# The second network's first layer as 2x2 block products by one level of Strassen's algorithm, with weights converted in pairs

## The chip, the core and the metric

One core of a Trainium2 chip runs the whole program. The metric is device microseconds of one execution, from launch to the end on the core; lower is better. Of the core's engines four compute: TensorE (PE: matmuls, results in PSUM; its weight loads are listed as PEld), VectorE (DVE), ScalarE (ACT) and GpSimd (POOL). SyncE's queue (SP) issues the transfers. Each engine works through its own queue in order, and an instruction whose semaphores have not been raised holds back everything behind it on that engine.

## What is computed

```python
def reference(q, k, v, w1, b1, w2, moe_..., moe2_...):
    x = _attn_ref(q, k, v, w1, b1, w2)      # B=2, H=8, S=576, D=64, bias by a small network
    x = x.transpose(0, 2, 1, 3).reshape(1152, 512)
    g = x @ w_gate; val = x @ w_val         # 512 -> 1536, the first network
    x = (silu(g) * val) @ w_out             # 1536 -> 512
    h = x @ w_in                            # 512 -> 2048, the second network's first layer
    return softplus(h) @ w_out2             # 2048 -> 512
```

The weights of both networks come as float64. Each product is made of three matmuls of a shorter kind (fp32r), which read operands that were rounded to it: for a = ah + al and b = bh + bl the kernel adds ah bh, ah bl and al bh.

## The kernel before

The core runs attention first, whose queues are written out by hand, then two networks on all 1152 tokens at once. X lies transposed, 512 features in four tiles of 128 partitions, tokens along the columns, as a high part `xh` and a low part `xl`.

**Weights.** `units` lists 68 blocks of 512 x 128 (or 128 x 512) float64 weights in the order of use: 24 for gate and value, 12 for the first network's output, and twice 8 for `w_in` with 8 for `w_out2`. `stages` (L511 to L531) turns one into float32 by bits and splits it: ScalarE scales the upper words by 2^-112 (L523), VectorE shifts left by 3 (L525), puts the sign bit back (L526) and adds three bits of the lower word (L528), ScalarE rounds to the high part `wh` (L530), GpSimd subtracts to get the low part `wl` (L531). `convert` and `weights` keep this some blocks ahead of their use; `ring` holds 9 blocks.

**Products.** `products` (L546) issues, for one block and one range of 384 tokens, 4 x 3 = 12 matmuls of 384 columns into one PSUM buffer (L552). The first network runs 12 feature blocks, each with gate and value on three token ranges; ScalarE's Silu, VectorE's product and `split` (high part L557 on ScalarE, low part L558 on VectorE) give `gh` and `gl`. Its output layer makes four rows of blocks, three weight blocks each, and `split` gives the next X, again as high and low part.

**Second network.** In two halves of 8 feature blocks: for each block and each token range 12 matmuls, Softplus (L609), `split` to `g2h` and `g2l`; then for each of nine blocks of 128 tokens 8 x 3 matmuls of 512 columns (L619), the result copied to or added to `acc` by VectorE (L623, L625), and in the second half sent out (L626). PSUM is 8 buffers of one bank (`psM`). Outside attention a scheduler orders each engine's queue ahead of the run, from the program's order and its own estimates; buffers are waited for tile by tile.

Of the kernel before, what the change touches and what calls it, by code (L numbers as in the profile page):

```python
# [19 lines left out]
P = 128  # L20
# [6 lines left out]
RING = 9  # L27
# [65 lines left out]
def tile_kernel(ctx: ExitStack, tc, qT, kT, vS, wb, wg, wv, wo, wi, wo2, table, out):  # L93
# [9 lines left out]
    def new_x():  # L103
        return [xp.tile([P, NK, NT], F32R, tag=t, name=t) for t in ("xh", "xl")]
# [8 lines left out]
    with ExitStack() as actx:  # L113
# [372 lines left out]
    units = []  # L486
    for f in range(FF1 // P):
        units += [col_block(wg, f), col_block(wv, f)]
    for m in range(NK):
        for fb in range(FF1 // P // NK):  # L490
            units.append(row_block(wo, fb, m))
    for hf in range(2):
        units += [col_block(wi, 8 * hf + f) for f in range(8)]
        units += [rows(wo2, 8 * hf + f) for f in range(8)]
    NU = len(units)

    mpool = opener(ctx)
    rawp = mpool("rawp", 3)
    cvp = mpool("cvp", 2)
    ring = mpool("ring", RING)  # L500
    wk = mpool("wk", 2)
    psM = mpool("psM", 8, space=PSUM)
    loaded, ready = [], []

    def load(n):
        while len(loaded) < min(n, NU):
            raw = rawp.tile([P, NK, P, 2], I32, tag="raw", name="raw")
# [156 lines left out]
```

## Time and profile before

| | |
|---|---|
| median of 3 runs | 620.9 us (620.18 to 623.96) |
| the profiled execution, its own time | 624.0 us |
| its span, first to last instruction | 622.2 us |
| TensorE busy | 606.4 us, 97% |
| VectorE / ScalarE / GpSimd busy | 391.5 / 312.3 / 195.9 us |
| first matmul of the first network | 195.58 us |
| first matmul of the second network | 420.60 us |
| last matmul starts | 618.24 us |

The profile is one execution on the chip. Busy time is the union of an engine's instructions; since matmuls overlap in the record (each lasts about twice its share), the pace of TensorE is read from the starts of successive matmuls, not from their durations. The same holds, less so, for VectorE and ScalarE, whose next instruction may start some 0.09 us before the last has ended.

### The profile page before, as it was taken

Reading aid. Unit: us, or ns where it says so; the run is one execution under the profiler, and the core shown is the slowest. Engines: PE = TensorE matmul, PEld = TensorE weight load, DVE = VectorE, ACT = ScalarE, POOL = GpSimd, SP = SyncE. Lnnn points to the kernel's source line nnn. Section 1 sums busy time; section 2 is a strip of 40 time slices with the busy share of each in tenths; the row PEclk is TensorE's granted clock in tenths of the full one; section 3 lists DMA queues with packets and bytes.
Section 4 is the critical chain, followed back from the end, with each engine's and each line's share of the span. In section 5 each row is a group of like instructions: output and inputs, shape, how many; then the busy total and the mean of one; then the engine's idle time right before and its main releaser. Section 6 shows DMA issues by size and latency. Waiting matters only on the chain.

```text
span 622.2 us, 10920 instructions
## 1 busy us (share of the span) xinstructions
PE 606.4 (97%) x4032; PEld 542.7 (87%) x4032; DVE 391.5 (63%) x849; ACT 312.3 (50%) x623; POOL 195.9 (31%) x231
## 2 busy tenths in 40 slices
PE   8899799999999999999999999999999999999997
PEld 5343588888888999999999999999998889999886
DVE  7999779999978996567566534325644017965111
ACT  5988767777776453434533332226662003675000
POOL 0301668888853441131121221212220004421000
PEclk9999889999999999999999999999999999999999
DMA  9879624444333553323323232323232003520111
GB/s 240 206 195 204 157 73 108 104 107 109 94 103 102 170 169 102 103 68 102 102 69 110 94 102 73 97 68 95 76 101 67 1 1 96 169 75 1 52 51 52
DMA packets 47413, 63.29 MB, mean 102 GB/s; under 512 B 4480, under 2 KB 35200, under 8 KB 47360
## 3 DMA queue, kind: packets, MB, share of 16 engines
q1 hardware_dynamic: 47360, 62.59, 35.6%
q8 instruction: 32, 0.52, 0.4%
q14 instruction: 21, 0.17, 0.1%
HBM read 49.60 MB, written 2.36 MB: 84 GB/s over the span
## 4 chain that ended last, share of the span: by engine, by line
PE 90%; DMA 3%; DVE 3%; ACT 2%; issue 1%; SPq 0%; POOL 0%; DVEq 0%; ACTq 0%; POOLq 0%
PE pm L552 52%; PE pm L619 16%; PE po L374 7%; PE ps L282 7%; PE pt L346 5%; PE pb L245 3%; DMA bias<-st 2%; DVE r L237 2%; ACT st L257 1%; PE warm L454 1%; DMA vt<-in_vS_dram 1%; ACT r L235 0%; PE ps L346 0%; SPq L142 0%; ACT at L354 0%
## 5 line engine op out<-in xcount | busy, mean ns | idle before, releaser
L531 POOL TENSOR_TENSOR wl<-x,wh 128x512 fp32r<-128x512 f32 x68 | 90.6, 1340 | 288.8 <-ACT wh L530 170.4
L552 PE MATMUL pm<-xh,wl 128*128 128x384 f32 x480 | 160.5, 334 | 0.0
L552 PE MATMUL pm<-xh,wh 128*128 128x384 f32 x480 | 160.4, 334 | 0.0
L552 PE MATMUL pm<-xl,wh 128*128 128x384 f32 x480 | 160.3, 334 | 0.0
L523 ACT ACTIVATE u<-raw 128x512 f32<-128x512 f32 x68 | 45.9, 675 | 107.1 <-DVE x L526 58.4
L552 PEld LDWEIGHTS pm<-xh,wh 128*128 128x128 f32 x480 | 90.1, 188 | 0.4 <-issue 0.4
L552 PEld LDWEIGHTS pm<-xh,wl 128*128 128x128 f32 x480 | 90.1, 188 | 0.3 <-POOL wl L531 0.3
L552 PEld LDWEIGHTS pm<-xl,wh 128*128 128x128 f32 x480 | 90.1, 188 | 0.0
L525 DVE TENSOR_SCALAR x<-u 128x512 int32<-128x512 int32 x68 | 41.5, 610 | 69.0 <-POOL wl L531 68.4
L530 ACT CAST wh<-x 128x512 fp32r<-128x512 f32 x68 | 42.1, 619 | 84.3 <-PE pm L619 40.2
L320 POOL TENSOR_SCALAR e<-e,sm 128x576 f32<-128x576 f32 x64 | 49.0, 766 | 41.0 <-DVE sm L319 28.9
L528 DVE SCALAR_TENSOR_TENSOR x<-raw,x 128x512 int32<-128x512 int32 x68 | 55.9, 822 | 1.5
L619 PE MATMUL pm<-wh,g2l 128*128 128x512 f32 x144 | 56.1, 389 | 0.0
L619 PE MATMUL pm<-wl,g2h 128*128 128x512 f32 x144 | 56.1, 389 | 0.0
L619 PE MATMUL pm<-wh,g2h 128*128 128x512 f32 x144 | 56.0, 389 | 0.0
L526 DVE SCALAR_TENSOR_TENSOR x<-u,x 128x512 int32<-128x512 int32 x68 | 54.0, 794 | 1.5
L245 PE MATMUL pb<-r,wb_sb 128*32 128x288 f32 x576 | 48.8, 412 | 6.1 <-ACT st L257 4.6
L317 ACT ACTIVATE e<-e,sm 128x576 f32<-128x576 f32 x64 | 49.9, 780 | 7.5 <-DVE sm L303 6.4
L282 PE MATMUL ps<-kst,ql 128*128 128x288 f32 x160 | 49.5, 338 | 4.2 <-DVE sm L318 2.3
L237 DVE TENSOR_SCALAR r<-G 128x576 f32<-128x576 f32 x108 | 51.4, 550 | 0.1
L303 DVE CUSTOM_DVE_ANT_0 e<-ps,bias 128x576 f32<-128x576 f32 x64 | 47.8, 747 | 2.1 <-ACT st L257 1.2
L245 PEld LDWEIGHTS pb<-r,wb_sb 128*32 128x32 f32 x576 | 20.2, 109 | 32.9 <-ACT st L257 13.6
(76 smaller groups left out, 1049.2 us busy)
## 6 DMA issues: line engine op xcount, KB each, us to landing
raw<-in_wo_dram SPq DMA_DIRECT2D x28, 512.0 KB, 3.5
bias<-st SPq DMA_DIRECT2D x32, 288.0 KB, 4.5
raw<-in_wi_dram SPq DMA_DIRECT2D x16, 512.0 KB, 3.7
raw<-in_wg_dram SPq DMA_DIRECT2D x12, 512.0 KB, 3.6
raw<-in_wv_dram SPq DMA_DIRECT2D x12, 512.0 KB, 3.6
kr<-in_kT_dram SPq DMA_DIRECT2D x16, 288.0 KB, 4.3
qr<-in_qT_dram SPq DMA_DIRECT2D x16, 288.0 KB, 4.3
v<-in_vS_dram SPq DMA_DIRECT2D x8, 384.0 KB, 4.9
```

The lines of the kernel that those rows point to most:

```text
L237: nc.vector.tensor_scalar(r, G[:, w0 : w0 + S], PB[:, n : n + 1], 0.0, op0=ALU.add, op1=ALU.max)
L245: nc.tensor.matmul(pb[32 * ct : 32 * ct + 32, hf, :HALF], W2, rs[ct][:, HALF * hf : HALF * (hf + 1)], start=True, stop=True,)
L282: nc.tensor.matmul(ps[:, hf, :HALF], u[t][:, o : o + P], kst[:, a, HALF * hf : HALF * (hf + 1)], start=i == 0, stop=i == len(parts) - 1,)
L303: nc.vector.tensor_tensor_reduce(out=e[:, :S].rearrange("p (a n) -> p a n", a=2), in0=ps[:, :, :HALF], in1=bt.rearrange("p (a n) -> p a n" ...
L317: nc.scalar.activation(e, e, AF.Exp, bias=sm[:, 0, n : n + 1], scale=-1.0, accum_out=sm[:, 1, n : n + 1])
L320: nc.gpsimd.tensor_scalar(e, e, sm[:, 3, n : n + 1], 1.0, op0=ALU.mult, op1=ALU.mult)
L523: nc.scalar.activation(u, hw.bitcast(F32), AF.Copy, scale=2.0**-112)
L526: nc.vector.scalar_tensor_tensor(x, ui, -(2**31), x, op0=ALU.bitwise_and, op1=ALU.bitwise_or)
L528: nc.vector.scalar_tensor_tensor(x, lw, 29, x, op0=ALU.logical_shift_right, op1=ALU.bitwise_or)
L531: nc.gpsimd.tensor_tensor(wl, x.bitcast(F32), wh.bitcast(F32), op=ALU.subtract)
L552: nc.tensor.matmul(ps[:, :n], w[:, k], x, start=first and k == 0 and i == 0, stop=last and k == NK - 1 and i == 2)
L619: nc.tensor.matmul(ps, g, w.rearrange("p k f -> p (k f)"), start=f == 0 and i == 0, stop=f == 7 and i == 2)
```

## The change

**Strassen.** The first layer of the second network, h = x @ w_in, is cut into 2 x 2 blocks: features in halves of 256, tokens in halves of 576, and output features in eight pairs of 128. For each pair (a *quad*) seven block products replace eight, in the form with shared sums (Winograd's): S1 to S4 are sums of weight blocks, T1 to T4 sums of X blocks. Each product is 2 x 3 x 2 = 12 matmuls of 288 columns (L702), the two halves of 576 columns in two banks of one buffer. Buffers of PSUM are now 4 of two banks (`wide`). The products x1 to x7 of a quad accumulate in three buffers a, b, c: x1 in a; c starts as a copy of a (L739, ScalarE); x5 and x3 in b; x6, x7 and x4 in c; results of b and c are kept (L728) and added (L722) where two outputs share them.

**Order.** TensorE's queue in the second network is written out by hand as words: x and y are the two quads of a round, z the next round's first, the digit the product, c a sum; t and u are the two halves of a block of tokens' output matmuls. There are four rounds of 2 quads and 4 x 128 features instead of two halves of 8 x 128. All other engines are still ordered by the scheduler.

**X.** The output layer of the first network writes X in full (`xf`, L654), and its blocks B and sums T, with high and low parts, are made as its rows finish (L619 to L628, L658 to L679).

**Weights.** They are converted two blocks at a time (`as_float`, 1024 columns; the first two pairs in halves). For the first network ScalarE's Prelu with slope -2^32 does the scaling and the sign in one instruction (L530), which takes out the sign instruction on VectorE; `w_in` and `w_out2` still have it (L535). The low parts are made by VectorE (`split`, L541); GpSimd has no instruction left behind attention. The ring holds 4 pairs, 6 in the second network. A quad also makes its four sums on VectorE (L558 to L561). The two explicit table loads are gone; ScalarE's queue has a load before the first Silu and before the first Softplus.

```diff
-        nc.scalar.activation(u, hw.bitcast(F32), AF.Copy, scale=2.0**-112)
-        nc.vector.tensor_scalar(x, ui, 3, None, op0=ALU.logical_shift_left)
-        nc.vector.scalar_tensor_tensor(x, ui, -(2**31), x, op0=ALU.bitwise_and, op1=ALU.bitwise_or)
-        nc.vector.scalar_tensor_tensor(x, lw, 29, x, op0=ALU.logical_shift_right, op1=ALU.bitwise_or)
-        nc.scalar.copy(wh, x.bitcast(F32))
-        nc.gpsimd.tensor_tensor(wl, x.bitcast(F32), wh.bitcast(F32), op=ALU.subtract)
...
+            if n < SLOPED:
+                nc.scalar.activation(y, hw.bitcast(F32), AF.Prelu, scale=2.0**-112, alpha=-(2.0**32))
+            else:
+                nc.scalar.activation(y, hw.bitcast(F32), AF.Copy, scale=2.0**-112)
+            nc.vector.tensor_scalar(yi, yi, 3, None, op0=ALU.logical_shift_left)
+            if n >= SLOPED:
+                nc.vector.scalar_tensor_tensor(yi, hw, -(2**31), yi, op0=ALU.bitwise_and, op1=ALU.bitwise_or)
+            nc.vector.scalar_tensor_tensor(yi, lw, 29, yi, op0=ALU.logical_shift_right, op1=ALU.bitwise_or)
...
+    def split(xh, xl, src):
+        nc.scalar.copy(xh, src)
+        nc.vector.tensor_tensor(xl, src, xh.bitcast(F32), op=ALU.subtract)
...
+            split(wh[:, 2:], wl[:, 2:], x[:, 2:])
+            tt(s[:, :2], x[:, :2], x[:, 2:4], op=ALU.add)
+            tt(s[:, 2:4], s[:, :2], x[:, 4:6], op=ALU.subtract)
+            tt(s[:, 4:6], x[:, 4:6], x[:, :2], op=ALU.subtract)
+            tt(s[:, 6:], x[:, 6:], s[:, 2:4], op=ALU.subtract)
+            split(sh, sl, s)
...
-            for o, n in TB:
-                xh, xl = x2
-                ps = psum()
-                products(ps, w, lambda k: (xh[:, k, o : o + n], xl[:, k, o : o + n]), n, True, True)
-                sg = wk.tile([P, 384], F32, name="sg")
-                nc.scalar.activation(sg[:, :n], ps[:, :n], AF.Softplus)
-                split(g2h[f][:, o : o + n], g2l[f][:, o : o + n], sg[:, :n])
...
+            for k in range(2):
+                xh, xl = X[x][k]
+                for i, (a, b) in enumerate(((wh, xh), (wh, xl), (wl, xh))):
+                    for hf in range(2):
+                        nc.tensor.matmul(
+                            ps[:, hf, :HALF],
+                            a[:, k],
+                            b[:, HALF * hf : HALF * (hf + 1)],
...
+        def p1(self):
+            self.a = wide()
+            self.product(self.a, "A11", "B11", start=True)
+
+        def p5(self):
+            self.b = wide()
+            self.product(self.b, "S1", "T1", start=True)
+            self.c = wide()
+            nc.scalar.copy(self.c[:, :, :HALF], self.a[:, :, :HALF])
+            self.five = self.kept(self.b)
+
+        def p2(self):
+            self.product(self.a, "A12", "B21")
+            self.out(0, 0, self.a)
+
+        def p6(self):
+            self.product(self.c, "S2", "T2")
+            self.two = self.kept(self.c)
...
+    FIRST = "x1 x5 x6 x3 xc y1 x2 x7 y5 y2 x4 y6 y3 yc"
+    OTHER = "x2 x6 x3 xc y1 x7 y5 y2 x4 y6 y3 yc"
+    TAIL = "t0 y7 t1 y4 u0 u1 t2 u2 t3 u3 z1 t4 u4 z5"
+    TOKENS = ((5, 6), (7, 8), (4, 0), (1, 2), (3,))
```

**Where the queues differ.** TensorE, at the first matmuls of the second network. Names: `pm`, `pw` are PSUM buffers with a number by tile, `xh` and `B11`, `T1`, `T2` the moving operand, `wh` and `wl` weights. Before:

```order
L552 MATMUL pm_4832<-gh11_2852,wl_4532 128x384
L552 MATMUL pm_4996<-xh_4309,wh_4579 128x384 [waits DVE_49]
L552 MATMUL pm_4996<-xl_4310,wh_4579 128x384
L552 MATMUL pm_4996<-xh_4309,wl_4580 128x384 [waits Pool_49]
L552 MATMUL pm_4996<-xh_4309,wh_4579 128x384 [waits Activation_49]
L552 MATMUL pm_4996<-xl_4310,wh_4579 128x384
L552 MATMUL pm_4996<-xh_4309,wl_4580 128x384
```

After:

```order
L702 MATMUL pw_4795<-B111_4134,wl_4558 128x288 x2
L702 MATMUL pw_4808<-T10_4135,wh_4559 128x288 [waits Activation_49]
L702 MATMUL pw_4808<-T10_4135,wh_4559 128x288 x3
L702 MATMUL pw_4808<-T10_4135,wl_4560 128x288 [waits DVE_49]
L702 MATMUL pw_4808<-T10_4135,wl_4560 128x288
L702 MATMUL pw_4808<-T11_4136,wh_4559 128x288 x4
L702 MATMUL pw_4808<-T11_4136,wl_4560 128x288 x2
L702 MATMUL pw_4821<-T20h_4618,wh_4559 128x288 [waits Activation_49]
L702 MATMUL pw_4821<-T20h_4618,wh_4559 128x288
L702 MATMUL pw_4821<-T20l_4619,wh_4559 128x288 [waits DVE_49]
```

Twelve matmuls of 384 columns for each token range have become products of twelve with 288, and the third product (into `pw_4821`) begins with a wait for ScalarE.

ScalarE at the same place, from the last row of blocks of the first network's output on. `xh_4309` and `xf3` take that row's results, `u` and `x` are weights under conversion, `B211h` and `T40h` high parts of X blocks, `sg` a Softplus. Before:

```order
L557 CAST xh_4309<-pm_4830 128x384 [waits PE_49]
L557 CAST xh_4309<-pm_4831 128x384 [waits PE_49]
L530 CAST wh_5153<-x_5152 128x512 [waits PE_49,Pool_49]
L530 CAST wh_5216<-x_5215 128x512 [waits DVE_49,PE_49,Pool_49]
L557 CAST xh_4309<-pm_4832 128x384 [waits PE_49]
L595 ACT_TABLE_LOAD
L523 ACTIVATE u_5403<-raw_5275 128x512 [waits DMAHW2_49,DVE_49,Activation_49]
L609 ACTIVATE sg_5009<-pm_4996 128x384 [waits PE_49]
L557 CAST g2h0_4980<-sg_5009 128x384 [waits Activation_49]
```

After:

```order
L654 COPY xf3_4132<-pw_4546 128x384 [waits PE_49]
L540 CAST wh_4774<-x_4766 128x768
L540 CAST B211h_4612<-xf3_4132 128x576 [waits Activation_49]
L540 CAST wh_4776<-s_4778 128x1024
L540 CAST T40h_4736<-s_4740 128x576 [waits DVE_49]
L739 COPY pw_4821<-pw_4795 128x2x288 [waits PE_49]
L540 CAST T41h_4738<-s_4745 128x576 [waits DVE_49]
L728 COPY kept_4823<-pw_4808 128x576 [waits PE_49]
L532 ACTIVATE x_4982<-raw_4767 128x1024 [waits DMAHW3_49,DMAHW4_49,DVE_49,Activation_49]
L728 COPY kept_4837<-pw_4821 128x576 [waits PE_49,Activation_49]
```

The copy that the third product waits for (L739, `pw_4821<-pw_4795`) stands behind five instructions that start when the output layer is done: the last piece of `xf3`, two weight roundings and two high parts of X.

ScalarE inside a round of the first layer. Before, in the first half:

```order
L523 ACTIVATE u_5466<-raw_5338 128x512 [waits DMAHW3_49,DVE_49]
L609 ACTIVATE sg_5026<-pm_5013 128x384 [waits PE_49]
L557 CAST g2h0_4980<-sg_5026 128x384 [waits Activation_49]
L530 CAST wh_5279<-x_5278 128x512 [waits PE_49,Pool_49]
L609 ACTIVATE sg_5043<-pm_5030 128x384 [waits DVE_49,PE_49]
L557 CAST g2h0_4980<-sg_5043 128x384 [waits Activation_49]
L609 ACTIVATE sg_5060<-pm_5047 128x384 [waits DVE_49,PE_49]
```

After, in the round behind the first:

```order
L540 CAST g2h0_5233<-s_5253 128x576 [waits Activation_49]
L728 COPY kept_5269<-pw_5229 128x576 [waits PE_49]
L717 ACTIVATE s_5283<-s_5283 128x576 [waits DVE_49]
L540 CAST g2h0_5233<-s_5283 128x576 [waits Activation_49]
L540 CAST wh_5573<-s_5575 128x1024 [waits DVE_49,PE_49]
L739 COPY pw_5331<-pw_5288 128x2x288
L717 ACTIVATE s_5313<-s_5313 128x576 [waits DVE_49]
L728 COPY kept_5333<-pw_5318 128x576 [waits PE_49]
L540 CAST g2h1_5235<-s_5313 128x576 [waits Activation_49]
```

Here the copy of the second quad (`pw_5331<-pw_5288`) stands behind the rounding of the next round's S blocks (`wh_5573`), which waits for TensorE to be done with the ring's old contents.

## Rows read from the trace of the kernel before

**Rows 1.** The page's first part: busy us (share of span), instructions.

```profile
PE 606.4 (97%) x4032; PEld 542.7 (87%) x4032; DVE 391.5 (63%) x849; ACT 312.3 (50%) x623; POOL 195.9 (31%) x231
```

**Rows 2.** Busy us (x count) by stretch: PE PEld DVE ACT POOL; clock, DMA, GB/s.

```profile
195.58:420.60 225.02, 225.02 (x1298) 224.73 (x1297) 136.74 (x214) 87.95 (x170) 56.19 (x43) 1.00 0.33 104
420.60:618.63 198.03, 198.03 (x1009) 180.76 (x1008) 85.89 (x135) 72.42 (x143) 33.11 (x24) 1.00 0.21 64
```

**Rows 3.** Waits of TensorE: who for whom, us in total, times, longest.

```profile
PEld pm L552 <- POOL wl L531: 0.3, 1, 0.3
```

**Rows 4.** TensorE's timeline, second network's first half: start, duration, instruction.

```profile
420.60 0.33 PE L552 MATMUL pm<-xh,wh 128*128 128x384 f32 x1
...
470.35 0.33 PE L552 MATMUL pm<-xh,wl 128*128 128x384 f32 x1
470.52 0.39 PE L619 MATMUL pm<-wh,g2h 128*128 128x512 f32 x1
...
519.52 0.33 PE L552 MATMUL pm<-xh,wh 128*128 128x384 f32 x1
```

**Rows 5.** TensorE's timeline in attention, scores of 288 columns.

```profile
122.29 0.29 PE L282 MATMUL ps<-kst,qh 128*128 128x288 f32 x1
...
122.69 0.38 PE L346 MATMUL pt<-ident,e 128*128 128x128 f32 x2
```

**Rows 6.** Weight loads by line: busy us, mean ns of one, idle before.

```profile
L552 PEld LDWEIGHTS pm<-xl,wh 128*128 128x128 f32 x480 | 90.1, 188 | 0.0
```

**Rows 7.** TensorE's timeline in attention, transposes of 128 columns.

```profile
190.02 0.27 PE L346 MATMUL ps<-ident,m 128*128 128x128 f32 x1
...
191.00 0.27 PE L346 MATMUL ps<-ident,e 128*128 128x128 f32 x1
```

**Rows 8.** VectorE's and GpSimd's timeline, POOL idle (269 us) and busy (527 us).

```profile
269.41 0.42 DVE L525 TENSOR_SCALAR x<-u 128x512 int32<-128x512 int32 x1
...
270.93 0.69 DVE L528 SCALAR_TENSOR_TENSOR x<-raw,x 128x512 int32<-128x512 int32 x1
271.54 0.55 DVE L578 TENSOR_TENSOR sg<-pm,sg 128x384 f32<-128x384 f32 x1
...
526.92 1.43 POOL L531 TENSOR_TENSOR wl<-x,wh 128x512 fp32r<-128x512 f32 x1 [2.99 <-ACT wh L530]
...
527.23 1.67 DVE L528 SCALAR_TENSOR_TENSOR x<-raw,x 128x512 int32<-128x512 int32 x1
```

**Rows 9.** Groups of instructions by shape: busy us, mean ns, idle before.

```profile
L531 POOL TENSOR_TENSOR wl<-x,wh 128x512 fp32r<-128x512 f32 x68 | 90.6, 1340 | 288.8 <-ACT wh L530 170.4
...
L525 DVE TENSOR_SCALAR x<-u 128x512 int32<-128x512 int32 x68 | 41.5, 610 | 69.0 <-POOL wl L531 68.4
...
L528 DVE SCALAR_TENSOR_TENSOR x<-raw,x 128x512 int32<-128x512 int32 x68 | 55.9, 822 | 1.5
...
L625 DVE TENSOR_TENSOR acc<-pm,acc 128x512 f32<-128x512 f32 x9 | 6.2, 691 | 41.8 <-PE pm L619 41.8
```

**Rows 10.** ScalarE: its timeline at 428 us, then groups by shape.

```profile
428.23 0.51 ACT L557 CAST g2h<-sg 128x384 fp32r<-128x384 f32 x1
428.65 0.61 ACT L530 CAST wh<-x 128x512 fp32r<-128x512 f32 x1
429.17 0.48 ACT L609 ACTIVATE sg<-pm 128x384 f32<-128x384 f32 x1
...
L257 ACT ACTIVATE st<-pb,G 128x576 f32<-128x576 f32 x36 | 26.5, 737 | 8.1 <-PE pb L245 4.7 <-DMA bias<-st 3.2
...
L609 ACT ACTIVATE sg<-pm 128x384 f32<-128x384 f32 x48 | 23.3, 485 | 4.8 <-PE pm L552 3.2 <-DVE g2l L558 1.6
...
L164 ACT CAST kst<-kr 128x576 fp32r<-128x576 f32 x8 | 5.3, 667 | 0.0
```

**Rows 11.** The end: TensorE's last matmul and its reader on VectorE.

```profile
618.24 0.39 PE L619 MATMUL pm<-wh,g2l 128*128 128x512 f32 x1
...
618.66 0.69 DVE L625 TENSOR_TENSOR acc<-pm,acc 128x512 f32<-128x512 f32 x1 [4.75 <-PE pm L619]
```

More of the change, by code (lines that the diff above doesn't have):

```diff
@@ L103, in new_x @@
     def new_x():
[L104 removed]
+        return [[xp.tile([P, NT], F32R, name=f"{t}{k}") for k in range(NK)] for t in ("xh", "xl")]
     xT = new_x()
@@ L481, in tile_kernel @@
                 run_slot()
[L486 to L495, printed above, removed]
+    pairs = [(col_block(wg, f), col_block(wv, f)) for f in range(FF1 // P)]
+    blocks = [row_block(wo, fb, m) for m in range(NK) for fb in range(FF1 // P // NK)]
@@ L533, in convert @@
[L533 to L544 removed]
+        while len(loaded) < min(n, len(pairs)):
+            raw = rawp.tile([P, 2 * NK, P, 2], I32, tag="raw", name="raw")
+            for i, src in enumerate(pairs[len(loaded)]):
+                half = raw[:, NK * i : NK * (i + 1)]
+                sp.dma_start(out=half.rearrange("p k f t -> p k (f t)"), in_=src)
+            loaded.append(raw)
@@ new lines, in tile_kernel, with pair, __init__, product @@
+    acc.append(accp.tile([P, 1, DM], F32, name="acc4"))
+    def pair(ap):
+        return ap.rearrange("p (a n) -> p a n", a=2)
+    class Quad:
+        def __init__(self, n):
+            convert(n + 1)
+            self.w = ready[n]
+        def product(self, ps, w, x, start=False):
+            wh, wl = self.w[w]
+            for k in range(2):
+                xh, xl = X[x][k]
[5 more added lines that the diff above has]
+                            b[:, HALF * hf : HALF * (hf + 1)],
+                            start=start and k == 0 and i == 0,
+                            stop=k == 1 and i == 2,
+                            skip_group_check=not start,
+                        )
+        def out(self, f, t, src):
+            gh, gl = [g[:, S * t : S * (t + 1)] for g in self.g[f]]
+            if src is None:
+                s = self.sums[f, t]
+            else:
+                s = row()
+            nc.scalar.activation(pair(s), pair(s) if src is None else src[:, :, :HALF], AF.Softplus)
+            split(gh, gl, s)
+        def total(self, f, t, ps, other):
+            s = row()
+            nc.vector.tensor_tensor(pair(s), ps[:, :, :HALF], pair(other), op=ALU.add)
+            self.sums = {(f, t): s}
+            self.out(f, t, None)
+        def kept(self, ps):
+            s = wk.tile([P, S], F32, tag="sg", name="kept")
+            nc.scalar.copy(pair(s), ps[:, :, :HALF])
+            return s
+        def p1(self):
[13 more added lines that the diff above has]
+            self.two = self.kept(self.c)
+        def p3(self):
+            self.product(self.b, "S4", "B22")
+        def c12(self):
+            self.total(0, 1, self.b, self.two)
+        def p7(self):
+            self.product(self.c, "S3", "T3")
+            self.total(1, 1, self.c, self.five)
+        def p4(self):
+            self.product(self.c, "A22", "T4")
+            self.out(1, 0, self.c)
```

238 lines of the change are left out of this document (163 added, 75 removed).

## Prediction

> **What bounds the kernel now.** I read the busy shares first: TensorE is busy 97% of the span, VectorE 63%, ScalarE 50% [rows 1]. An average hides stages, so the next view is busy time by stretch. From 195.58 us, the first matmul of the first network, to 618.63 us TensorE is busy in every microsecond of both stretches, at granted clock 1.00, its 2.4 GHz level, while VectorE is busy 85.89 us of the 198.03 us in which the second network runs [rows 2]. The table of waits then lists one TensorE wait there, 0.3 us for the first weights, and nothing later [rows 3]. So whatever shortens TensorE's queue behind 195.58 us shortens the span, as long as nobody else becomes late.
>
> The matmul timeline gives the pace. From 420.60 to 470.52 us 288 matmuls of 384 columns start, so one each 0.17333 us; the next 216, of 512 columns, take 49.00 us, 0.2268 us each [rows 4]. 384 columns at 2.4 GHz are 0.160 us, 512 are 0.2133: each instruction costs 13.3 ns beside its columns.
>
> **What is removed from TensorE.** The first layer of the second network had 16 blocks x 3 column ranges x 12 = 576 matmuls: 576 x 0.17333 = 99.84 us. It becomes 8 quads x 7 products x 12 = 672 matmuls of 288 columns. The trace has this shape in attention: three score matmuls of 288 columns in a row and the next instruction start over 0.40 us [rows 5], 0.133 us each, and 288 / 2.4 GHz + 13.3 ns is the same 0.1333 us. 672 x 0.1333 = 89.60 us. **Term 1: -10.24 us.** Token matmuls (432) and the first network's (1296) keep count and shape; pieces of 6 or 12 in another order cost nothing by themselves, since the change of shape at 470.52 us shows no gap [rows 4].
>
> Beside that pace stands a page's rule: the Trainium skill (TensorE: Matmul & The Clock Gate, Back-to-back issue gap) gives a warm gap of columns / 2.4 plus 2.5 ns. By it the layer goes from 93.6 to 82.3 us, a gain of 11.3 us; here 384 columns take 173.3 ns and not 162.5, so the trace disagrees and the sum keeps 10.24.
>
> Does a load of weights limit the shorter matmul? Loads are recorded at 188 ns, longer than the pace, so they overlap [rows 6]; attention's 128-column transposes, a load each, start 0.109 us apart (9 in 0.98 us) [rows 7]. 0.1333 is above that, so no.
>
> **Weights: VectorE takes over low parts, POOL falls silent.** A GpSimd subtraction takes 1340 ns in the mean, and holds VectorE: an instruction that takes 0.69 us alone takes 1.67 us while one runs [rows 8, 9]. Behind attention the change leaves POOL nothing, so I use undisturbed VectorE times: two-input instructions 0.55 us for 384 columns and 0.69 for 512, about 1.05 ns a column, next start 0.08 us before the end; the one-input shift 0.42 us for 512 [rows 8]. In start-to-start time that is 0.34 us for 256 columns, 0.68 for 576, 0.88 for 768, 1.15 for 1024, and 0.61 for a 1024 shift.
>
> One of the four rounds (two quads, two pairs of output weights, nine token blocks) then costs VectorE:
> - a quad's weights: 0.61 + 2 x 1.15 + 0.88 + 4 x 0.34 + 1.15 = 6.3 us, twice 12.6;
> - an output pair: 0.61 + 3 x 1.15 = 4.1 us, twice 8.1;
> - results: per quad two sums and four low parts, 6 x 0.68 = 4.1, twice 8.2;
> - nine accumulations at 0.61 (0.69 long) [rows 9]: 5.5.
>
> Sum 34.4 us, against TensorE's 168 x 0.1333 + 108 x 0.2268 = 46.9 us a round: 73%. ScalarE starts the next instruction 0.42 us after one of 384 columns and 0.52 after 512, and a 576 cast lasts 667 ns, some 0.58 to the next start [rows 10]; with the same 0.83 ns a column that is 0.74 for 768 and 0.96 for 1024. It needs per quad 1.0 + 0.74 + 0.96 + 11 x 0.58 = 9.1 us and per pair 2.0: 22 us a round. Both fit, so these edits cost nothing while TensorE has 46.9 us to cover them.
>
> In the first network a pair costs VectorE 0.61 + 1.15 + 1.15 and its three results 6 x 0.47, 5.7 us within 72 x 0.1733 = 12.5 us. Prelu in Copy's place has no row; by Softplus's 485 ns for 384 columns, less than a cast's 0.51 [rows 10], I take the price of a cast. It would need several microseconds more a pair to show; the order has three table loads, as before. The preparation of X (B11, T1 to T4, ...) is some 9 us of ScalarE and 15 us of VectorE, under the output layer's 75 us of matmuls but for what needs its last block.
>
> **Where TensorE newly waits.** Results reach ScalarE or VectorE about 0.2 us after the next matmul could start: the last matmul starts at 618.24, its slot ends at 618.47, and its reader starts at 618.66 [rows 11].
>
> (a) Start of the layer. Put 0 at the end of the last output matmul's slot. x1 and x5 (24 matmuls) run to 3.20 us; x6 accumulates on a copy of x1's result that ScalarE makes (L739). ScalarE's queue ahead of it, as order shows: `xf3` piece 0.20 to 0.62, `wh` 768 to 1.36, `B211h` to 1.94, `wh` 1024 to 2.90, `T40h` to 3.48, copy to about 4.15. A PSUM-to-PSUM copy has no row; Softplus reads 384 columns from PSUM in 485 ns (645 at 576), and a copy of 576 with a scale by partition takes 737 [rows 10]; I take 667 ns, as for the cast. Ended at 4.15 for 3.20: **1.0 us**. Behind the copy wait `T41h`, the two kept copies and a table load; x3 is then due at 5.8 and its kept copy done at 5.4, y2 is due at 13.85 and its copy done at 13.6, so nothing follows. A copy 0.1 us shorter or longer moves this by as much; the bounds are 0 (copy first in the queue) and 2 us.
>
> (b) Rounds 1 and 2, counted from 0. y2 is due 9.60 us into the round (x2 x6 x3 y1 x7 y5) and needs the copy of y1's result. Ahead of it a 1024 cast waits for x7's end, 8.0 + 0.2: 8.2 to 9.16, then the copy to 9.83. **0.25 us, twice.** Round 3 has no such cast.
>
> (c) The others have slack: token blocks t0 at 16.0 have weights since about -0.8 and results since 12; u0 at 24.64 has y7's low part (ends 20.3, then sum, Softplus, cast, low part) at 23.5, 1.1 us early; x7 at 6.4 has its kept copy at 4.1. The output layer needs a PSUM buffer back 2.1 us after each row of blocks, and ScalarE frees it 1.4 us after (0.2, a 768 cast 0.74, a copy 0.48): no wait. Loads are the same bytes. The one wait of before, on GpSimd's first low part, may go; I count nothing for it.
>
> **Sum.** -10.24 + 1.0 + 0.5 = -8.7; for slack that I counted too well another 0.3: **-8.4 us**. The span of 622.2 becomes 613.8. The profiled execution took 624.0 us with what lies around its span; that is 3.1 above the median of the three runs, 620.9. A difference of the queue carries over: 620.9 - 8.4 = **612.5 us**.
>
> **Rivals.**
> - *Copies late in every quad.* Each quad has the wait of (a), because ScalarE's copy stands behind other work in its queue: 8 x 1.0 instead of 1.5 loses 6.8, 619.2 us. For: the copy is never first in the queue and slacks of 0.2 to 1.1 us are thin. Against: in steady rounds x's copy ends 3 us early. At 1.28 us a quad nothing is gained. Cases from 614.7 to 621: 0.17.
> - *VectorE binds.* With disturbed prices (610 ns for 420, 822 for 688 [rows 8, 9], up to 1.45 times) a round costs 49.9 us for 46.9: 3.0 us in each of the three rounds that also prepare the next one's weights, and (a) and (b): 620.9 - 10.24 + 9.0 + 1.5 = 621.2. Against: POOL has no instruction there. 0.05.
> - *Slower: weight loads bind.* In long rows of 288 columns the 188 ns loads no longer hide; attention shows only four in a row. If a matmul stays at 0.1733 us, 672 take 116.5 us, +16.6: 637.5 us. It decides from 0.1486 us a matmul. Against: the transposes' 0.109 us. 0.05, with smaller slips past 627.
> - *Faster: shared weights.* The two halves of a product use one set of weights. If the second loads nothing and saves the 13.3 ns, 336 x 13.3 = 4.5 us: 608.0. Against: now (wh, xl) follows (wh, xh) with the same weights, and still has a load for each of its 480 matmuls [rows 6], at no shorter pace. 0.08. A fixed cost per matmul smaller than 13.3 ns at this width lies between this and the forecast, within the same chance. The gap rule of the Trainium skill (TensorE: Matmul & The Clock Gate) is such a case: by it, 611.4 us.
>
> **Numbers.** The forecast (copies and casts wait about as worked out, 610.5 to 614.7) has 0.65. This kernel's runs tell about 1%, 6.2 us, from no change. Faster by over 1%, under 614.7: forecast and shared weights, 0.73. Same: late copies and VectorE, 0.22. Slower: 0.05. The range 608.0 to 618.5 leaves out the slow ends of late copies and the last cases, under 0.2.
>
> **What will show it.** L702's matmuls 0.133 us apart, 672 of them; one TensorE wait of about 1 us on L739's copy at the layer's start, small ones twice later; VectorE busy about 34 us (40 with overlaps counted) in a round of 47, at 1.2 us for 1024 columns; POOL idle behind attention; L530's Prelu near 1.1 us. I am wrong if 288-column matmuls start further apart than 0.14 us, or if waits of TensorE on ScalarE or VectorE add up to more than 4 us.

## The result and the profile after

The changed kernel takes 612.76 us (median of four runs, 612.21 to 614.52) where the kernel before, beside it, takes 621.13: a ratio of 0.9863 with a 95% interval of 0.9825 to 0.9901, 8.4 us or 1.4% faster. The prediction was 612.5 us. The profiled execution took 614.52 us, its span is 612.6.

The page's first part, busy us (share of the span) and instructions, answers [rows 1]:

```profile
PE 597.5 (98%) x4128; PEld 532.4 (87%) x4128; DVE 416.1 (68%) x843; ACT 333.1 (54%) x579; POOL 106.0 (17%) x163
```

TensorE has 96 matmuls more and is busy 8.9 us less; VectorE and ScalarE have more to do, and GpSimd's 106 us all lie in attention. Busy time by stretch (PE, PEld, DVE, ACT, POOL; clock, DMA share, GB/s) answers [rows 2]: the first network, then the four rounds of the second.

```profile
194.72:420.06 225.34, 225.34 (x1298) 225.34 (x1297) 113.22 (x166) 86.84 (x140) 0.00 (x0) 1.00 0.29 94
420.06:465.23 45.17, 44.43 (x266) 40.39 (x265) 42.40 (x57) 30.82 (x41) 0.00 (x0) 1.00 0.29 94
465.23:512.21 46.98, 46.98 (x277) 42.64 (x276) 38.49 (x50) 23.50 (x32) 0.00 (x0) 1.00 0.43 135
512.21:559.20 46.99, 46.99 (x278) 42.64 (x276) 35.65 (x47) 23.49 (x32) 0.00 (x0) 1.00 0.14 46
559.20:612.60 53.40, 49.78 (x289) 44.66 (x287) 19.20 (x26) 16.33 (x24) 0.00 (x0) 0.99 0.12 45
```

A steady round takes 46.98 us, and TensorE is busy in all of it. Its waits behind 195 us (who for whom, us in total, times, longest) are one place, seen by its two queues; they stand where [rows 3] had the wait for GpSimd:

```profile
PEld pw L702 <- ACT pw L739: 1.0, 1, 1.0
PE pw L702 <- ACT pw L739: 0.7, 1, 0.7
```

TensorE's timeline there, the first three products (start, duration, instruction, idle before), answers [rows 4]:

```profile
420.06 0.69 PE L702 MATMUL pw<-B,wh 128*128 128x288 f32 x4
...
421.65 0.69 PE L702 MATMUL pw<-T,wh 128*128 128x288 f32 x4
...
422.99 0.42 PE L702 MATMUL pw<-T,wl 128*128 128x288 f32 x2
424.15 0.53 PE L702 MATMUL pw<-T20h,wh 128*128 128x288 f32 x2 [0.74 <-ACT pw L739]
424.52 0.43 PE L702 MATMUL pw<-T20l,wh 128*128 128x288 f32 x2
```

x1 takes 1.59 us for twelve matmuls. x6 was due at 423.26 and starts at 424.15, and its first two matmuls take 0.37 us instead of 0.27: 1.0 us lost. ScalarE's timeline shows why:

```profile
420.26 0.48 ACT L654 COPY xf<-pw 128x384 f32<-128x384 f32 x1 [1.55 <-PE pw L573]
420.63 0.84 ACT L540 CAST wh<-x 128x768 fp32r<-128x768 f32 x1
421.37 0.68 ACT L540 CAST B211h<-xf 128x576 fp32r<-128x576 f32 x1
421.94 1.05 ACT L540 CAST wh<-s 128x1024 fp32r<-128x1024 f32 x1
422.89 0.67 ACT L540 CAST T40h<-s 128x576 fp32r<-128x576 f32 x1
423.46 0.64 ACT L739 COPY pw<-pw 128x576 f32<-128x576 f32 x1
```

ScalarE is not idle for a moment; the copy simply stands sixth.

From the first to the last start of a matmul the second network takes 188.53 us (420.06 to 608.59) for 197.64 before [rows 4, 11]: **-9.11 us**. The rest of the difference of the two profiled spans (9.6 us) lies ahead of it: the first network starts 0.86 us earlier and takes 0.3 us longer. Attention moves by such amounts from run to run, so below the length of the second network, start to start, stands beside each ratio. Each ratio is to runs of before on the same chip, whose medians were 621.1 to 622.6 us.

### The profile page after: what moved, and what is told of

It is laid out like the page before. It is cut to its first block, busy times and chain, and to the rows that moved or that the text cites. A ratio compares the mean times of both kernels' runs of the same rounds, so it can differ in the third digit from the quotient of the medians.

```text
span 612.6 us, 10748 instructions
## 1 busy us (share of the span) xinstructions
PE 597.5 (98%) x4128; PEld 532.4 (87%) x4128; DVE 416.1 (68%) x843; ACT 333.1 (54%) x579; POOL 106.0 (17%) x163
## 4 chain that ended last, share of the span: by engine, by line
PE 88%; DMA 4%; ACT 3%; DVE 2%; issue 1%; SPq 1%; POOL 0%; DVEq 0%; ACTq 0%; POOLq 0%
PE pw L573 37%; PE pw L775 16%; PE pw L702 14%; PE po L376 7%; PE ps L284 7%; PE pt L348 5%; DMA bias<-st 3%; PE pb L247 2%; DVE r L239 2%; ACT st L259 1%; ACT r L237 1%; DMA vt<-in_vS_dram 1%; DMA G<-in_table_dram 1%; ACT wh L540 0%; PE ps L348 0%
## 5 line engine op out<-in xcount | busy, mean ns | idle before, releaser
L573 PE MATMUL pw<-xh,wh 128*128 128x384 f32 x288 | 96.3, 334 | 0.0
L573 PE MATMUL pw<-xl,wh 128*128 128x384 f32 x288 | 96.2, 334 | 0.0
L573 PE MATMUL pw<-xh,wl 128*128 128x384 f32 x288 | 96.2, 334 | 0.0
L540 ACT CAST wh<-x 128x1024 fp32r<-128x1024 f32 (+2 forms) x36 | 34.4, 956 | 84.3 <-PE pw L573 38.0
L541 DVE TENSOR_TENSOR wl<-x,wh 128x1024 fp32r<-128x1024 f32 (+2 forms) x36 | 39.7, 1103 | 57.0 <-ACT wh L540 56.9
L775 PE MATMUL pw<-wh,g2h 128*128 128x512 f32 x144 | 56.2, 390 | 0.0
L775 PE MATMUL pw<-wh,g2l 128*128 128x512 f32 x144 | 56.1, 390 | 0.0
L775 PE MATMUL pw<-wl,g2h 128*128 128x512 f32 x144 | 56.1, 389 | 0.0
L573 PEld LDWEIGHTS pw<-xh,wh 128*128 128x128 f32 x288 | 54.1, 188 | 0.4 <-issue 0.4
L319 ACT ACTIVATE e<-e,sm 128x576 f32<-128x576 f32 x64 | 49.9, 780 | 8.1 <-DVE sm L305 6.2
L573 PEld LDWEIGHTS pw<-xl,wh 128*128 128x128 f32 x288 | 54.1, 188 | 0.0
L573 PEld LDWEIGHTS pw<-xh,wl 128*128 128x128 f32 x288 | 54.1, 188 | 0.0
L573 PE MATMUL pw<-gh,wh 128*128 128x384 f32 x144 | 48.4, 336 | 0.0
```

What stands on the lines that cost most here:

```text
L319: nc.scalar.activation(e, e, AF.Exp, bias=sm[:, 0, n : n + 1], scale=-1.0, accum_out=sm[:, 1, n : n + 1])
L541: nc.vector.tensor_tensor(xl, src, xh.bitcast(F32), op=ALU.subtract)
L573: nc.tensor.matmul(ps[:, :n], w[:, k], x, start=first and k == 0 and i == 0, stop=last and k == NK - 1 and i == 2)
L775: nc.tensor.matmul(ps, g, w.rearrange("p k f -> p (k f)"), start=f == 0 and i == 0, stop=f == 3 and i == 2)
```

## Experiments

| kernel | second network, us | median, us | ratio to before (95%) |
|---|---|---|---|
| before | 197.64 | 621.13 | 1 |
| changed | 188.53 | 612.76 | 0.9863 (0.9825 to 0.9901) |
| e0 changed, again | 188.50 | 613.93 | 0.9868 (0.9845 to 0.9891) |
| e1 weight edits alone | 197.64 | 621.51 | 0.9990 (0.9977 to 1.0003) |
| e3 an eighth product | 202.09 | 625.27 | 1.0040 (1.0025 to 1.0055) |
| e10 weights alternate | 188.76 | 614.16 | one run |
| e4 T4 later | 187.98 | 612.78 | 0.9852 (0.9833 to 0.9871) |
| e9 T4 later, y1 earlier | 189.14 | 613.59 | 0.9852 (0.9830 to 0.9874) |
| e5 copy made three times | 209.76 | 633.96 | 1.0172 (1.0153 to 1.0191) |
| e6 one VectorE instruction more a pair | 189.47 | 613.95 | 0.9851 (0.9836 to 0.9867) |
| e7 two more a pair | 189.74 | 613.56 | 0.9843 (0.9822 to 0.9863) |
| e2 low parts on GpSimd | 200.74 | 626.39 | 1.0070 (1.0052 to 1.0088) |
| e11 only the quads' low parts | 195.12 | 619.88 | 0.9981 (0.9959 to 1.0003) |
| e8 GpSimd beside, nobody waits | 196.93 | 620.69 | 0.9966 (0.9946 to 0.9985) |

### Is it the matmuls? (e0, e1, e3, e10)

> The changed kernel once more, to be compared with the other runs of this group. The change is worth -9.1 us by the two traces (second network 197.64 us of matmul starts before, 188.53 after), so a ratio near 0.986, 612 to 613 us. If the gain were an accident of the one profiled execution, the ratio would be above 0.990.

Measured: 188.50 us and 0.9868. The gain stands.

e1, in the kernel before:

```diff
-        nc.scalar.activation(u, hw.bitcast(F32), AF.Copy, scale=2.0**-112)
+        sloped = i < 36
+        if sloped:
+            nc.scalar.activation(u, hw.bitcast(F32), AF.Prelu, scale=2.0**-112, alpha=-(2.0**32))
...
-        nc.gpsimd.tensor_tensor(wl, x.bitcast(F32), wh.bitcast(F32), op=ALU.subtract)
+        nc.vector.tensor_tensor(wl, x.bitcast(F32), wh.bitcast(F32), op=ALU.subtract)
```

> The kernel before with the weight edits alone: low parts on VectorE, signs of the first network's and its output's weights by Prelu; single blocks, no Strassen. My theory (TensorE is the only bound behind 195 us, weights are hidden): no change, 620.5 to 621.5 us, the one wait of 0.3 us for a low part at most gone. Rival (part of the gain comes from GpSimd no longer holding VectorE): 2 us or more faster. Rival (VectorE gets late with results): TensorE waits of over 1 us, slower than 622.

Measured: 0.9990, and a second network of 197.64 us, to the hundredth that of before. TensorE's timeline of e1, first and last matmul of the second network:

```profile
417.81 0.33 PE L557 MATMUL pm<-xh,wh 128*128 128x384 f32 x1
...
615.45 0.39 PE L624 MATMUL pm<-wh,g2l 128*128 128x512 f32 x1
```

So the weight edits alone bring nothing.

e3, in the changed kernel:

```diff
             self.product(self.c, "S3", "T3")
+            self.product(self.c, "S3", "T3")
```

> The changed kernel with the seventh product of each quad issued twice (its result is then counted twice), so that a quad has eight products as without Strassen. Theory (TensorE is the bound and a product costs its twelve matmuls of 288 columns): 8 x 12 x 0.1333 = 12.8 us more, second network 201.3 us; that is more than before's 197.6, since 768 matmuls of 288 columns cost 2.6 us more than 576 of 384. The waits stay those of the changed kernel. Rival (other engines set the rounds): 6 us more or less, since a product is partly hidden.

Measured: 13.6 us more in the second network. 12.8 are the matmuls; 0.8 is lost at the first round's u0, whose sixth matmul waits for a low part of results that VectorE has not finished. TensorE's timeline of e3:

```profile
452.38 0.50 PE L776 MATMUL pw<-wh,g2l 128*128 128x512 f32 x1 [0.49 <-DVE g2l L541]
```

The time lies above before's: at this width the eighth product, which Strassen's algorithm saves, costs 12.8 us, and the narrower matmuls take 2.6 of the saving back.

e10, in the changed kernel, turns the loop over the halves `hf` outward:

```diff
-            for k in range(2):
-                xh, xl = X[x][k]
-                for i, (a, b) in enumerate(((wh, xh), (wh, xl), (wl, xh))):
-                    for hf in range(2):
+            for hf in range(2):
+                for k in range(2):
+                    xh, xl = X[x][k]
+                    for i, (a, b) in enumerate(((wh, xh), (wh, xl), (wl, xh))):
```

> The changed kernel with the two halves of a product one after the other instead of in turn, so that each matmul has other weights than the one before. Theory (a load for each matmul is hidden, 288 columns cost 0.133 us with or without the same weights): second network 188.5 us, no change. Rival (the halves share a load that would otherwise not hide): above 0.14 us a matmul, 4.5 us more or above.

Measured: 188.76 us in one run, with matmuls still 0.133 us apart; the 0.2 us more lie at y2 of rounds 1 and 2, which starts 0.13 us late. Two matmuls with the same weights cost what two with different ones cost. The rival "shared weights" falls.

### Where the copies stand (e4, e9, e5)

e4 puts L672 to L679, which make T4 and B21's second half, into a function `last_blocks` and calls it behind x5 instead of ahead of the layer. By that ScalarE's copy (here L741) moves from sixth to fourth place, counted with `xf`'s last piece.

```diff
+                if q == 0 and word == "x5":
+                    last_blocks()
```

> The changed kernel with the X blocks that are needed last (T4 and the second half of B21) issued in the program behind the fifth product instead of ahead of the layer, so that ScalarE's copy for the third product is the third instruction behind the output layer instead of the sixth. Theory: the copy ends at 2.9 us of the layer instead of 4.0, the product is due at 3.2, its wait of 1.0 us goes and nothing else appears: 1.0 us faster than the changed kernel (ratio lower by 0.0016), second network 187.5 us. Rival (the same work is only late elsewhere, as at the second quad's product y2, which has 0.3 us of slack in the first round): a new wait of TensorE of up to 1 us there, no gain.

Measured: 187.98 us, 0.5 less than e0 and not 1.0. ScalarE's timeline of e4:

```profile
419.35 1.05 ACT L540 CAST wh<-s 128x1024 fp32r<-128x1024 f32 x1
420.30 0.64 ACT L741 COPY pw<-pw 128x576 f32<-128x576 f32 x1
420.87 0.67 ACT L540 CAST B211h<-xf 128x576 fp32r<-128x576 f32 x1
421.44 1.15 ACT L532 ACTIVATE x<-raw 128x1024 f32<-128x1024 f32 x1
422.49 0.61 ACT L730 COPY kept<-pw 128x576 f32<-128x576 f32 x1
```

The copy ends at 420.94, before x6 is due at 421.23, and x6 does not wait. But now a weight conversion of 1.15 us has slipped in ahead of the next copy, which x3 waits for (TensorE's timeline of e4):

```profile
423.16 0.53 PE L704 MATMUL pw<-B220h,wh 128*128 128x288 f32 x2 [0.17 <-ACT kept L730]
```

x3 was due at 422.83; 0.43 us are given back, 0.33 of waiting and 0.10 of a slow start. By the medians of one chip e4 lies 1.15 us below e0, but the intervals overlap, so only the traces tell the two apart.

e9 also puts y1 between x6 and x3:

```diff
-    FIRST = "x1 x5 x6 x3 xc y1 x2 x7 y5 y2 x4 y6 y3 yc"
+    FIRST = "x1 x5 x6 y1 x3 xc x2 x7 y5 y2 x4 y6 y3 yc"
```

> The run with T4 later left a wait of 0.4 us at x3, whose kept copy stands behind a weight conversion on ScalarE. Here y1 (12 matmuls, 1.6 us) is put between x6 and x3 as well. Theory: x3 is due 1.6 us later and its copy long done, y1's low part is done 1 us before it is due; second network 187.6 us for 188.0 with T4 later and 188.5 for the changed kernel. That is 0.15% from the changed kernel. Rival (y2's copy gets behind more): a new wait of up to 1 us at y2 in the first round, no gain.

Measured: 189.14 us, worse than the changed kernel. The wait at x3 is gone, and the rival came instead. The timeline of e9 there, ScalarE and TensorE:

```profile
431.20 0.68 ACT L719 ACTIVATE s<-s 128x576 f32<-128x576 f32 x1 [0.82 <-DVE s L724]
431.79 0.63 ACT L741 COPY pw<-pw 128x576 f32<-128x576 f32 x1
...
432.48 0.53 PE L704 MATMUL pw<-B210h,wh 128*128 128x288 f32 x2 [1.30 <-ACT pw L741]
```

The copy for y2 stands behind a Softplus that waits for VectorE's sum. Neither move brings a gain that the runs can tell; the best trace is e4's.

e5 makes the copy three times, with other work of ScalarE's queue in between:

```diff
             nc.scalar.copy(self.c[:, :, :HALF], self.a[:, :, :HALF])
+            for _ in range(2):
+                nc.scalar.copy(self.c[:, :, :HALF], self.a[:, :, :HALF])
```

> The changed kernel with ScalarE's copy of x1 into the third buffer made three times; the queue puts two to four instructions of 0.57 us between the first and the third. Theory (read from the slack of each copy in the trace of the changed kernel): x6 at the layer's start waits 2.3 us longer, y2 of the four rounds waits 2.4, 2.2, 2.2 and 0.6 us longer, x6 of rounds 1 to 3 has 2.7 us of slack and does not wait: 9.7 us more, about the time of the kernel before. Rival (each quad is at its edge): 8 x 2.3 = 18 us more. Rival (VectorE is what the quads wait for): 3 us more or less.

Measured: 21.2 us more in the second network. My 9.7 was wrong in two ways. First, x in rounds 1 to 3 does wait, 1.5 us each: the copy reads x1's buffer, and x2, which comes one product ahead of x6, overwrites it. So the slack there is not x6's 2.7 us but x2's 1.15 (copy done at 469.99, x2 due at 471.14 in the changed kernel). With 3.1, 1.5, 2.3, 1.5, 2.3, 1.5 and 0.7 us at the other products and 2.25 more at the layer's start the waits make 15 us. Second, TensorE is slow behind the longest of them. Its timeline in e5 at the first round's y2:

```profile
439.01 0.85 PE L702 MATMUL pw<-B210h,wh 128*128 128x288 f32 x2 [2.93 <-ACT pw L741]
...
440.13 0.68 PE L702 MATMUL pw<-B210h,wl 128*128 128x288 f32 x2
440.61 0.68 PE L702 MATMUL pw<-B211h,wh 128*128 128x288 f32 x2
```

Busy time by engine in the stretch from there, then the clock, the DMA share and GB/s:

```profile
438.85:446.00 7.15, 6.99 (x32) 7.00 (x33) 4.17 (x5) 3.82 (x7) 0.00 (x0) 0.57 0.11 38
```

Two matmuls start 0.48 us apart instead of 0.267, 0.24 each, which is 288 columns at 1.2 GHz, from 439.0 to 444.9; the granted clock of the stretch is 0.57. This adds 2.7 us to a wait of 3.1. The wait at the layer's start, as long, is followed by 3.1 us at this pace (1.4 us lost), the one at round 1's y2 by some 3 us; over the layer it makes some 6 us.

### What covers the weight work (e6, e7, e2, e11, e8)

e6 and e7 repeat, for the second network's pairs, VectorE's last instruction (L536), which changes nothing when it is made again, once in e6 and twice in e7:

```diff
             nc.vector.scalar_tensor_tensor(yi, lw, 29, yi, op0=ALU.logical_shift_right, op1=ALU.bitwise_or)
+            for _ in range(1 if n >= NF1 + NK * (NF1 // NK) // 2 else 0):
+                nc.vector.scalar_tensor_tensor(yi, lw, 29, yi, op0=ALU.logical_shift_right, op1=ALU.bitwise_or)
```

> The changed kernel with the last of VectorE's instructions on a pair of weights (the or with the lower word, which changes nothing when repeated) made twice in the second network: 4 x 1.15 = 4.6 us more VectorE work in a round, 39 of 47 us. Theory (a round has 12 us to spare on VectorE): at most 1 us more. Rival (VectorE's queue is already what the copies and buffers wait for, as the run with GpSimd's low parts suggests): 3 to 18 us more, with waits of TensorE on copies that wait for accumulations.

> The same with the instruction made three times: 9.2 us more in a round, 43.6 of 47 us on VectorE, the same load as GpSimd's low parts with the time that they hold VectorE (42.7), but without GpSimd. If the load and the order of VectorE's queue alone cost the 12 us of that run: some 10 us more here too, with a wait of 5 us at the second quad's or first quad's x6 in a round. If it was GpSimd's longer low part (2.4 us against 1.2) that held back the conversions: at most 3 us more.

Measured: 0.9 and 1.2 us more by the traces, nothing that the medians show. In e7 VectorE is busy 44 to 45 us of 47 in each of the first three rounds. Its stretches for rounds 1 and 2, where the changed kernel has 38.5 and 35.7:

```profile
466.00:513.00 47.00, 46.60 (x274) 41.99 (x273) 44.15 (x56) 23.66 (x32) 0.00 (x0) 1.00 0.28 90
513.00:560.00 47.00, 47.00 (x277) 42.40 (x277) 44.90 (x57) 23.95 (x33) 0.00 (x0) 1.00 0.28 90
```

Over the whole second network VectorE is busy 165.1 us, for 135.0 in the changed kernel. The cover that the prediction named is real: 30 us of VectorE work can be added under TensorE for 1.2 us. One condition goes with it: in the trace of e7 ScalarE's and VectorE's queues stand in another order than in the changed kernel, since the scheduler orders them with the added instructions in the program. The same load in an unchanged order was not tried.

e2 undoes the weight edits and keeps the rest (`split` gets the engine of the low part as a parameter, the pairs' split too):

```diff
-    SLOPED, QUADS = len(pairs), {}
+    SLOPED, QUADS = 0, {}
...
-            split(wh[:, 2:], wl[:, 2:], x[:, 2:])
+            split(wh[:, 2:], wl[:, 2:], x[:, 2:], nc.gpsimd)
...
-            split(sh, sl, s)
+            split(sh, sl, s, nc.gpsimd)
```

> The changed kernel with the weight edits undone: low parts of weights back on GpSimd, Copy and a sign instruction on VectorE for all weights; pairs and Strassen stay. Theory: GpSimd works some 15 us and VectorE 28 + 15 us of a round of 47, both hidden, so the time of the changed kernel within 0.6 us, with VectorE instructions beside GpSimd's longer (up to 1.7 us for 0.7). Rival (VectorE would bind without the edits): 3 us a round and more, 620 us or above.

Measured: 12.2 us more in the second network and 1.2 in the first: slower than before the change. My theory falls here. The rival's time came, but not for its reason: in its second network VectorE is busy 135.1 us, in that of the changed kernel 135.0. The largest loss is at round 1's x2: TensorE waits 4.91 us for the copy, and the copy for VectorE. The timeline of e2 there, GpSimd, VectorE and ScalarE:

```profile
466.70 2.40 POOL L541 TENSOR_TENSOR wl<-s,wh 128x1024 fp32r<-128x1024 f32 x1 [3.83 <-ACT wh L540]
...
467.62 2.03 DVE L533 TENSOR_SCALAR x<-x 128x1024 int32<-128x1024 int32 x1 [2.14 <-ACT x L532]
...
474.54 2.77 POOL L541 TENSOR_TENSOR wl<-x,wh 128x1024 fp32r<-128x1024 f32 x1 [5.44 <-ACT wh L540]
...
475.14 3.25 DVE L536 SCALAR_TENSOR_TENSOR x<-raw,x 128x1024 int32<-128x1024 int32 x1
...
478.31 1.87 DVE L803 COPY acc<-pw 128x512 f32<-128x512 f32 x3
...
479.62 0.62 ACT L739 COPY pw<-pw 128x576 f32<-128x576 f32 x1 [5.23 <-DVE acc L803]
```

The copy needs the PSUM buffer of token block t3. Its accumulations (L803) stand in VectorE's queue behind two conversions, which keep VectorE busy from 467.62 on. They start 9.0 us after the block's last matmul (its slot ends at 469.32), where in the changed kernel they start 0.7 us after it (465.93 for 465.23). Two instructions of the conversions last longer beside GpSimd's subtractions, 2.03 us for 0.69 and 3.25 for 1.22. By these differences the hold makes some 3.4 of the 9.0 us (my estimate), and the order of the queue the rest. Behind this wait TensorE again runs at a granted clock of 0.50 for 5.4 us.

e11 leaves to GpSimd only the low parts of the quads' weights (none of the first network's own weights; that is what the expectation's clause on the first network means).

> The changed kernel with GpSimd making the low parts of the second network's first-layer weights alone (per quad 768 and 1024 columns, 9 us of GpSimd a round); the output weights' low parts stay on VectorE, the first network keeps Prelu, its low parts go to GpSimd too only for the first layer's quads, not for its pairs. VectorE's queue puts the accumulations of token block t3 behind both conversions at a round's end, as in the run with all low parts on GpSimd. If that order with conversions held back by GpSimd (each frees its buffer 1.2 us later) made the wait of 5 us on x's copy there: 5 to 10 us more than the changed kernel. If it takes the holds of the output weights' low parts too: at most 3 us more.

Measured: 6.6 us more. 2.1 are at the place named, x's copy in round 1. The larger part I had not named; it is at the layer's start. The timeline of e11 there, of all four engines:

```profile
419.56 2.29 POOL L541 TENSOR_TENSOR wl<-x,wh 128x768 fp32r<-128x768 f32 x1 [23.10 <-DVE s L677]
...
420.07 2.39 DVE L541 TENSOR_TENSOR B211l<-xf,B211h 128x576 fp32r<-128x576 f32 x1
...
421.81 2.90 POOL L541 TENSOR_TENSOR wl<-s,wh 128x1024 fp32r<-128x1024 f32 x1
...
422.39 2.93 DVE L678 TENSOR_TENSOR s<-s,T21l 128x576 f32<-128x576 f32 x1
...
425.35 0.67 ACT L540 CAST T41h<-s 128x576 fp32r<-128x576 f32 x1 [3.29 <-DVE s L678]
425.93 0.63 ACT L728 COPY kept<-pw 128x576 f32<-128x576 f32 x1
...
426.62 0.53 PE L702 MATMUL pw<-B220h,wh 128*128 128x288 f32 x2 [2.63 <-ACT kept L728]
```

Two VectorE instructions of 0.75 us last 2.4 and 2.9 beside two GpSimd subtractions. ScalarE's T41h waits for the second, and the kept copy that x3 needs stands behind T41h, although it needs neither. x3 starts 2.8 us late, and a spell of TensorE at half its clock costs another 1.5. This is one chain through four engines, and VectorE, the one that is late, is busy little longer than in the changed kernel (138.1 us of the second network, for 135.0).

e8 keeps the changed kernel's work and the order of VectorE's and ScalarE's queues, and has GpSimd subtract each high part from itself, to no use:

```diff
+        for i in range(xh.shape[1]):
+            t = xh[:, i].bitcast(F32)
+            nc.gpsimd.tensor_tensor(idle, t, t, op=ALU.subtract)
```

> The changed kernel, low parts on VectorE as they are, with GpSimd subtracting each high part of weights from itself into an unused tile, 128 columns at a time: some 15 to 20 us of GpSimd a round, as with its low parts, which hold VectorE but on which nobody waits; the order of VectorE's and ScalarE's queues is that of the changed kernel. If GpSimd's hold on VectorE made the 12 us of the run with GpSimd's low parts: 6 to 12 us more here, with TensorE waits of several us on copies. If it was what that run changes in the queues (accumulations behind the next pair's conversion, which waits for GpSimd to free its buffer): at most 1.5 us more, as with one or two VectorE instructions more.

Measured: 8.4 us more by the trace, 0.9966. GpSimd's group from 420 us on (busy us, mean ns, idle before):

```profile
L547 POOL TENSOR_TENSOR idle<-wh 128x128 f32<-128x128 f32 x162 | 120.9, 746 | 59.5 <-ACT wh L541 47.5
```

TensorE's waits in e8's second network, in total, times, longest:

```profile
PE pw L711 <- ACT pw L748: 4.2, 4, 1.8
PE pw L711 <- ACT kept L737: 1.8, 1, 1.8
```

In its trace both queues stand in the order of the changed kernel, and in the second network no wait is put down to GpSimd. So the hold alone makes such waits. It was twice as much GpSimd time as in e2 (121 us for 55) for less loss, though in shorter pieces; that e2 lost more by the order of VectorE's queue is shown at its largest wait and argued for the rest. How the 12 us divide between these was not separated.

## Why the prediction was right, and where not

**The bound and the pace: right.** TensorE is busy throughout, and the sum of its matmuls explains the layer. Where one matmul of 288 columns follows another without a loss, 653 of them start 0.1330 us apart in the mean; 0.1333 was taken from three in attention [rows 5]. Term 1 was -10.24 us; with it alone the second network would take 187.40 us, and the trace has 188.53. The 1.13 us more are 1.0 at x6 and 0.18 at y2, to within 0.05. The Trainium skill (TensorE: Matmul & The Clock Gate, Back-to-back issue gap) gives N / 2.4 + 2.5 ns for N columns, as the gap of an isolated matmul; for 288 columns that is 122.5 ns. The trace has 10 ns more for each matmul in a row, so the gain of 11.3 us by the formula did not come.

**Changes of shape: right.** Twelve token matmuls between products take 2.74 us for 2.72 in long rows.

**(a) The wait for the copy: right, in place, cause and size.** Predicted 1.0 us, measured 0.89 and 0.10. The copy from PSUM to PSUM lasts 635 ns (667 taken), the queue ahead of it ended at 3.40 us for 3.48.

**(b) y2 in rounds 1 and 2: right place, wrong size.** Predicted 0.25 us each, measured 0.09. The timeline of after in round 1, ScalarE and TensorE:

```profile
479.06 1.05 ACT L540 CAST wh<-s 128x1024 fp32r<-128x1024 f32 x1 [0.47 <-PE pw L702]
480.01 0.63 ACT L739 COPY pw<-pw 128x576 f32<-128x576 f32 x1
...
480.72 0.51 PE L702 MATMUL pw<-B210h,wh 128*128 128x288 f32 x2
```

The cast waits for x7's matmuls to be done with the ring's weights. I gave it the 0.2 us by which results of TensorE come late. But it needs no result, only the place of weights that have been used: it starts 0.06 us before x7's last slot ends (479.12, twelve slots ahead of y2). With the 0.3 us for miscounted slack, which did not occur, the sum should have been -9.1, as the traces have it, and not -8.4. That the median came out at -8.4 all the same is luck, within the scatter of runs (the interval is -10.9 to -6.1 us).

**(c) Slack: right in the result, wrong in one reason.** "x's copy ends 3 us early" in steady rounds took x6 as the one who waits. It is x2, by what it overwrites, and the slack is 1.15 us; e5 showed it, where x2 of rounds 1 to 3 came 1.5 us late each time.

**Durations: right.** Prelu on 1024 columns takes 1133 ns (1.1 predicted); the low part of 1024 on VectorE 1223; the third round, which has just the 47 VectorE instructions of the sum, keeps VectorE busy 35.7 us, 34.4 predicted, and a steady round keeps ScalarE busy 23.5, 22 predicted. The first two rounds have leftovers beside these (42.4 and 38.5 us), and the last has no weights to convert (19.2). Groups of instructions by shape (busy us, mean ns, idle before), which answer [rows 9, 10]:

```profile
L541 DVE TENSOR_TENSOR wl<-x,wh 128x1024 fp32r<-128x1024 f32 x24 | 29.4, 1223 | 47.5 <-ACT wh L540 47.5
...
L530 ACT ACTIVATE x<-raw 128x1024 f32<-128x1024 f32 x16 | 18.1, 1133 | 13.5 <-DVE wl L541 10.2 <-DMA raw<-in_wv_dram 3.3
...
L739 ACT COPY pw<-pw 128x576 f32<-128x576 f32 x8 | 5.1, 635 | 0.0
```

**"These edits cost nothing while TensorE has 46.9 us to cover them": right for VectorE's added work, wrong as a reading of the edits.** e7 shows the cover. But I read the move of the low parts as neutral and priced its opposite by shares (a round of 49.9 us for 46.9). e2 and e11 show that in the changed kernel it is worth 7 to 13 us, and by another mechanism: single instructions held until they last 2 to 3 us, and accumulations further back in VectorE's queue, at places where the chain from VectorE over ScalarE's copies to TensorE has 0 to 1.2 us of slack. Before the change the same edits are worth nothing (e1). There no product waits for a copy, and a subtraction has 512 columns and not 1024; which of the two counts is not shown, since Strassen's products with single blocks of weights were not tried. The change is a pair of edits, of which the second pays only beside the first.

**The rivals.** Late copies came at one place of eight (at all eight, by the prediction's own terms, they would have cost 6.5 us and 619.0; the 6.8 and 619.2 are slips), VectorE does not bind (e6, e7), weight loads do not bind, and shared weights bring nothing (e10). That each quad stands near its edge was closer to the truth than its 0.17 said: e5 made seven more quads wait with 2.3 us of delay.

## What to carry to other kernels

When matmuls bind, price a change by the count and the pace of matmuls from rows of the same width, and then look for the first instruction of each product that waits for another engine: what stands ahead of the releaser in its queue, and who else overwrites what it reads. A busy share of 70% says that added work fits, not that a hold of 2 us fits; for that the slack of each chain counts. An edit that measures as nothing on the old kernel can be a condition of the new one, so undo it there, too.

## What the runs showed of the hardware

- A spell of TensorE at half its clock (0.50 granted, 1.2 GHz) follows some waits, and the length of the wait alone does not tell which. Behind 2.93 us in e5 the matmuls of 288 columns started 0.24 us apart for 5.9 us, behind 2.99 us in the same run for 3.1, behind 4.91 us in e2 for 5.4. At the first round's x3 a wait of 2.63 us in e11 was followed by such a spell of 3.4 us, one of 2.64 us at the same place in e2 by none. Behind 1.80 us in e8 there was one, behind 1.88 us in e11 none; behind 2.10 us in e5 once and once not; behind 1.35 us and less never. What decides it was not tried; a wait of 3 us can cost 6.
- GpSimd's subtraction held VectorE's instructions with two operands in SBUF until it ended: 0.75 us became 2.39 and 2.93 in e11, and both end 0.6 us behind the subtraction. The Trainium skill (SBUF — State Buffer, Who interferes with whom) says that such an instruction contends with one of GpSimd that reads SBUF, and these rows agree. VectorE's shift, with one operand, was held too (e2, 2.03 us for 0.69).
- An instruction that only needs weights released can start 0.06 us before the slot of the last matmul that uses them ends, where a reader of results comes 0.2 us behind it [rows 11].
